# Attention and gated MLP block on one core: chunk ranks, bank-emptying rank, prologue engines and 217 instead of 200 VectorE exponential tiles

## The chip, the cores and the metric

The kernel runs on one core of a Trainium2 chip, in one launch. The metric is the device time of that launch in microseconds (us). A core has a matrix engine (TensorE, PE in the profile), VectorE (DVE), ScalarE (ACT), GpSimd (POOL) and a queue that issues transfers (SyncE, SP). TensorE writes into eight banks of PSUM of 128 x 512 fp32 each, and the other engines empty them.

## The reference

A pre-norm attention block with 32 heads of width 20 over 2048 tokens of width 640, and behind it a gated MLP of width 1728. All inputs are bfloat16.

```python
x = A_x                                   # (1, 2048, 640)
qkv = layernorm(x) @ wqkv                 # 32 heads, Dh = 20
s   = einsum("bhqd,bhkd->bhqk", q, k) * Dh ** -0.5
o   = einsum("bhqk,bhkd->bhqd", softmax(s), v)
h   = x + o.reshape(B, S, D) @ wo
n   = layernorm(h)
out = h + (gelu_tanh(n @ w_gate) * (n @ w_up)) @ w_down
```

## The kernel before

**Scores and exponentials.** The queries are cut into seven chunks of 512, 512, 256, 256, 256, 128 and 128 rows (`CHUNKS`), and the work of a chunk into slots of 64 tiles, 32 slots in all. A tile is 128 keys by 512 columns of scores, one PSUM bank; a group of heads is four heads, whose scores run in four row groups of TensorE. Tiles are put together into units of two or three (`PATS`: a slot marked 2 alternates 3 and 2 banks, a slot marked 3 alternates 3 and 3, and then leaves the background only one bank instead of two). ScalarE takes the exponential of a whole unit in one activation, from 128x1024 or 128x1536, into `pts` or the part of `rege` called `pts2`. `DS` says in hexadecimal how many of a slot's three-tile units give their third tile to VectorE (`d_exp`): one raw step from PSUM per tile, and then seven steps on SBUF for each pair of tiles. The exponentials multiply V on TensorE, accumulated in bank 6, and `epilogue` divides by the sum.

**Behind the attention.** `post` does the rest of a chunk: residual rows of x into `h_sb`, transposed attention output, projection `wo`, LayerNorm (`ln_stats`, `ln_rsqrt`, `ln_apply`), transposes, gates (copied to SBUF, line 1046, then gelu on ScalarE, which needs another activation table than the exponentials), ups (multiplied in line 1058) and downs (added in line 1074, then stored). `h_sb` and the buffer of the gates have room for four tiles of 128 rows: chunks 0 and 1 fill it, chunks 2 and 4 share rows 0 and 1, chunk 3 has rows 2 and 3, chunk 5 row 2 and chunk 6 row 3. The last chunk's `post` is the tail: its gates go from PSUM straight through gelu, line 1032, with ups interleaved in line 1035. The MLP's weights are loaded over the weights of the Q, K and V projections, so after the last of these (`w_readers`).

**What sets the order.** Each operation is recorded with an engine, a planned duration and a rank (line 353 and the other helpers), and `Sched.schedule` then runs a plan: on each engine, among what is ready, the lowest rank first, and within a rank the first recorded. The result is a fixed order for each engine, joined by semaphores. Ranks: scores and their exponentials `P_QK` 0, value products `P_PV` 1, epilogue `P_EPI` 2, background `P_BG` 3, gelu -1, VectorE's seven steps `DPR` 2. All of `post` before the tail has rank 3 (lines 950, 976, 979 and `mms`), so an older chunk's ups and downs, recorded first, go before a younger chunk's projection, LayerNorm and gates. A background operation is put on TensorE only if it ends before a due time, which is when the next unit's scores must start: the later of its banks coming free and ScalarE's coming free less a margin (line 153). Where TensorE would idle for long, the plan puts in a dummy matmul on `gk` (`idle`).

**Prologue.** x comes in four transfers of 512 rows. For each tile of 128 rows LNS says which engine makes the statistics, LNE which one normalizes, LNV which one copies the transposed tile out of PSUM. Group 0's K and Q are then projected (`proj`, ranks G0P, engines G0E for the copy), and V's first half in two banks (`proj_v`).

Of the kernel before, what the change touches and what calls it, by code (L numbers as in the profile page):

```python
# [20 lines left out]
LATE = (0, 1, 2, 3, 4)  # L21
LNS = [{'a': 'act', 'd': 'dve'}[x] for x in 'ddaadddddddaddaa']
LNE = [{'a': 'act', 'd': 'dve'}[x] for x in 'aaaaaaaaddaddddd']
LNV = [{'a': 'act', 'd': 'dve'}[x] for x in 'ddddadaaadaaadad']
SLIP = 0.0
# [25 lines left out]
class Sched:  # L51
# [3 lines left out]
    def __init__(self, nc):  # L55
        self.nc = nc
        self.ops = []
        self.lw = {}
        self.rd = {}

    def op(self, eng, fns, dur, prio, reads=(), writes=(), acq=(), rel=(), after=(), sem=None, lat=None, mode=None, mb=0.0, alt=None):
        o = Op()
        o.i = len(self.ops)
        o.eng, o.dur, o.lat, o.sem = eng, dur, LAT[eng] if lat is None else lat, sem
        o.mode = mode
        o.mb = mb
        o.alt = alt
        o.tag = writes[0] if writes else None
        o.fns = fns if isinstance(fns, list) else [fns]
        o.prio = (prio, o.i)  # L70
        deps = set(after)
        for r in reads:
            if r in self.lw:
                deps.add(self.lw[r])
        for w in writes:
            if w in self.lw:
                deps.add(self.lw[w])
            deps.update(self.rd.get(w, ()))
        for r in reads:
            self.rd.setdefault(r, []).append(o.i)  # L80
        for w in writes:
            self.lw[w] = o.i
            self.rd[w] = []
        deps.discard(o.i)
        o.deps = deps
        o.acq = list(acq)
        o.rel = list(rel)
        o.succ = []
        o.ready = 0.0
        o.start = None  # L90
        o.group = None
        self.ops.append(o)
        return o.i

    def schedule(self):
# [24 lines left out]
        while done < len(ops):  # L120
# [4 lines left out]
            for e in ENGINES:  # L125
# [9 lines left out]
                while ready[e]:  # L135
# [11 lines left out]
                    if got is None:  # L147

                        if p[0] == 0:
                            kept.update(bk.allowed[0] for bk in o.acq)  # L150
                            if e == "pe" and due is None and all(owner[bk.allowed[0]] is None for bk in o.acq):
                                due = max(max(free_at[bk.allowed[0]] for bk in o.acq),
                                          free["act"] - LOOK - o.dur - LAT["pe"])
                        skipped.append((p, i))
                        continue
# [168 lines left out]

P_QK, P_PV, P_EPI, P_BG = 0, 1, 2, 3
TFIRST = 0.0
PRE = 0.0
G0P = (1.5, 2.2, 2.5, 0.5, 2.2)
G0E = [{'a': 'act', 'd': 'dve'}[x] for x in 'aaaad']


def bass_sequential_preLN__mha_block__glu_gated_geglu__prompt_kernel(
# [12 lines left out]
    with ExitStack() as es:  # L345
# [115 lines left out]
        def cst(fn, key, n=128):  # L461
            op(POOL, fn, 0.1 + n * 0.001, P_BG, writes=[key, "pool"])

        cst(I("memset", ident[:], 0.0), "ident")
        cst(I("affine_select", out=ident[:], in_=ident[:], compare_op=ALU.not_equal, fill=1.0,
# [17 lines left out]
        cst(I("memset", e0[:], 0.0), "e0", 1)  # L483
        cst(I("memset", off0[:], 0.0), "off0", 1)
        for j in range(4):
            cst(I("memset", gqh[32 * j:32 * j + 21, 32 * j:32 * j + 1], -0.5), "gqh", 1)
            cst(I("memset", e0[32 * j:32 * j + 1, :], 1.0), "e0", 1)
            cst(I("memset", off0[32 * j:32 * j + 1, :], OFF), "off0", 1)
        pvb0 = Bank(6)
# [4 lines left out]
        def load(dst, src, key, mb, after=(), writes=None):  # L494
            return op("sp", I("dma_start", dst, src), 0.3, P_BG, writes=writes or [key], after=after, sem=key, mb=mb)

        def load_x(i):
            load(x_sb[:, 4 * i:4 * i + 4, :], x_hbm[512 * i:512 * (i + 1), :].rearrange("(t p) d -> p t d", p=128),
                 f"x{i}", 0.65)

# [5 lines left out]

        e_ops = []

        pad_ops = []
# [20 lines left out]
        def ln_stats_act(src, t, rkeys, prio):  # L530
            op("act", I("activation", xn_t[:, t % 2, :], src, ACT.Identity, scale=1.0 / D, accum_out=mv[:, t, 0:1]), 0.65, prio,
               reads=rkeys, writes=[("mv0", t), ("xnj", t % 2)])
            op("act", I("activation", xn_t[:, t % 2, :], src, ACT.Square, bias=mv[:, t, 0:1], scale=-1.0, accum_out=mv[:, t, 1:2]),
               0.65, prio, reads=list(rkeys) + [("mv0", t)], writes=[("mv1", t), ("xnj", t % 2)])

# [40 lines left out]
        def transposes(src, rkeys, dst, wkey, banks, prio, evac, after=(), al=tuple(range(NA)), dma=False, first_=False):  # L576
            if DT and dma:
                aft = tuple(after) + tuple(sc.rd.get(wkey, ()))
                for a in range(NA):
                    op("sp", I("dma_start", dst[:, a, :], src[:, a * 128:(a + 1) * 128], transpose=True), 0.06, prio,  # L580
                       reads=rkeys if len(rkeys) < NG or first_ else rkeys[0:(a * 128 + 127) // 80 + 1], writes=[wkey] if a == NA - 1 else [(wkey, a)], sem=f"t{wkey[1]}", lat=2.6, after=aft)
                return
# [9 lines left out]
            if evac == "act":  # L592
                op("act", lambda eng: eng.activation(dst, v(), ACT.Copy), c_act(128 * len(al)), prio, reads=[key],  # L593
                   writes=[wkey], rel=[bk], after=after)
            else:
                op("dve", lambda eng: eng.tensor_copy(dst, v()), c_dve(128 * len(al)), prio, reads=[key], writes=[wkey],
                   rel=[bk], after=after)
# [10 lines left out]
        for t0 in range(0, NT, 4):  # L608
            sa = [t for t in range(t0, t0 + 4) if LNS[t] == "act"]
            for t in range(t0, t0 + 4):  # L610
                (ln_stats_act if t in sa else ln_stats)(x_sb[:, t, :], t, [f"x{t // 4}"], P_EPI)
            if sa:
                assert sa == list(range(sa[0], sa[-1] + 1))
                op("dve", I("tensor_scalar", mv[:, sa[0]:sa[-1] + 1, 1], mv[:, sa[0]:sa[-1] + 1, 1], 1.0 / D, None, ALU.mult), 0.14,
                   P_QK, reads=[("mv1", t) for t in sa], writes=[("mv", t) for t in sa])
            ln_rsqrt(t0, 4, P_QK, 1)
            for t in range(t0, t0 + 4):
                e_ops.append(ln_apply(LNE[t], x_sb[:, t, :], xn_p[:, t % 4, :], ("xnp", t % 4), t, [f"x{t // 4}"], P_QK))
                transposes(xn_p[:, t % 4, :], [("xnp", t % 4)], xnT[:, :, t * 128:(t + 1) * 128], ("xnT", t),
                           ALLB, P_EPI, LNV[t])  # L620
                e_ops.append(len(sc.ops) - 2)
# [84 lines left out]

        def proj_v(kt, hf, banks, prio, evac="dve"):
            bk = Bank(*banks)
# [9 lines left out]
            else:  # L718
                op("dve", lambda eng: eng.tensor_copy(dst, src()), c_dve(320), prio, reads=[key],  # L719
                   writes=[("v", kt, hf)], rel=[bk])  # L720

# [13 lines left out]

        PATS = '22222222322222232222332222222332'
        DS = '06408846766698a67985888788668802'
        PAT = [((0, 1, 2), (3, 4, 5)) if PATS[i] == '3' else ((0, 1, 2), (3, 4)) for i in range(len(slots))]
# [210 lines left out]
        def post(c, banks, tail):  # L949
            p = P_EPI if tail else P_BG - PRE * (c >= len(CHUNKS) - 2)  # L950
            q0, nq = CHUNKS[c]
# [9 lines left out]
            for tt in range(nt):  # L961
# [7 lines left out]
                else:  # L969
                    transposes(o_nat[:, tt, :], [("on", g) for g in range(NG)], oT[:, :, ht * 128:(ht + 1) * 128],  # L970
                               ("hnT", ht), banks, P_EPI, "dve", after=first, dma=True, first_=c == 0)
                for hf in range(2):
                    bk = Bank(*banks)
                    key = ("bk", sc_id())
                    list(chain(bk, key, 320, [(oT[:, a, ht * 128:(ht + 1) * 128], wo[:, a, hf * 320:(hf + 1) * 320])
                                              for a in range(NA)], [("hnT", ht), "wo"] + [("oTa", ht)] * tail, p))
                    op("dve", lambda eng, bk=bk, ht=ht, hf=hf: eng.tensor_tensor(
# [10 lines left out]
            for tt in range(nt):  # L988
                t = q0 // 128 + tt
                ln_apply("dve", h_sb[:, hb + tt, :], xn_t[:, t % 2, :], ("xn", t % 2), t, [("h", hb + tt, 0), ("h", hb + tt, 1)], p)  # L990
                transposes(xn_t[:, t % 2, :], [("xn", t % 2)], hnT[:, :, (hb + tt) * 128:(hb + tt + 1) * 128], ("hnT", hb + tt),
                           banks, p, "dve", after=first, dma=not tail)
            p, pre = P_BG - TFIRST * tail, p
# [92 lines left out]
        for kt in range(NT):  # L1086
            proj_v(kt, 0, (6, 7), P_BG, "dve")
        ui = 0
        for s_, (c, gs) in enumerate(slots):
            if c == 0:  # L1090
# [5 lines left out]
                if g < 3:  # L1096
                    for kt in range(NT * g // 3, NT * (g + 1) // 3):
                        proj_v(kt, 1, BG0, P_BG)
                if g == 5:
# [60 lines left out]
```

## Time and profile before

| what | value |
|---|---|
| median of 3 runs | 959.46 us (959.09 to 959.96) |
| the profiled execution | 959.65 us |
| its span in the profile | 957.6 us |
| TensorE busy | 888.7 us, 93% |
| ScalarE busy | 910.2 us, 95% |
| VectorE busy | 771.6 us, 81% |
| dummy matmuls on `wo,gk` | 374, 65.7 us |
| ScalarE table loads | 15, 19.2 us |

Times are those of one profiled execution. Records of ScalarE and VectorE overlap their neighbours a little, so the mean length of a record is more than what an instruction adds on a full engine; for that the starts of neighbouring records are compared. In a row of the timeline the columns are start, length, engine, line, operation, output and input, count, and in brackets the idle time before it with what ended it. Where several instructions are merged into one row, the shape shown is that of the first.

### The profile page before, as it was taken

To read this page: it belongs to the slowest core of one execution; us is meant where nothing else is said; L and a number is where in the kernel's file an instruction comes from. 1 tells how busy PE (TensorE), PEld (TensorE's weight loads), DVE (VectorE), ACT (ScalarE), POOL (GpSimd) and SP (SyncE) were. 2 spreads that over 40 slices of the span, in tenths; PEclk is the share of its full clock that TensorE was granted. 3 is DMA by queue.
4 is the path that set the end of the run, shared out by engine and by line. 5 is a ranking of instruction groups with operands and counts; after the bars stand their busy time and mean duration, and the time that the engine had idled before them with its cause. 6 is when DMAs were issued, how large, how long until landed. Compare 5 with 4: busy or idle time off the path is not lost.

```text
span 957.6 us, 33012 instructions
## 1 busy us (share of the span) xinstructions
PE 888.7 (93%) x15035; PEld 391.2 (41%) x15038; DVE 771.6 (81%) x1705; ACT 910.2 (95%) x879; POOL 17.4 (2%) x54
## 2 busy tenths in 40 slices
PE   4999999999999999999999999799999999899998
PEld 2433332232322333233344433334444555655667
DVE  6659758998989998989779989689899978775543
ACT  7799999999999999999999999999999999999931
POOL 4200000000000000000000000000000000000000
PEclk9999999999999999999999999999999999999999
DMA  7000000000000700000001000000110000000000
GB/s 247 2 29 2 2 1 1 2 1 2 1 1 3 262 18 2 1 1 2 9 16 37 2 3 2 1 2 2 30 31 2 3 3 11 24 18 18 4 9 22
DMA packets 11755, 19.88 MB, mean 21 GB/s; under 512 B 544, under 2 KB 9696, under 8 KB 11616
## 3 DMA queue, kind: packets, MB, share of 16 engines
q1 hardware_dynamic: 11616, 17.78, 5.5%
q8 instruction: 118, 1.93, 0.8%
q14 instruction: 21, 0.17, 0.1%
HBM read 15.16 MB, written 2.62 MB: 19 GB/s over the span
## 4 chain that ended last, share of the span: by engine, by line
ACT 90%; PE 7%; DVE 1%; DMA 1%; issue 0%; SPq 0%
ACT pts L353 52%; ACT rege L353 36%; PE ps L632 4%; PE ps L636 1%; ACT L353 1%; PE ps L353 1%; DMA rege<-in_A_x_dram 1%; ACT xn_t L353 0%; DVE rege L353 0%; DVE sq L353 0%; DVE v_all L719 0%; PE ps L586 0%; ACT regw L593 0%; DVE qt_all L667 0%; SPq L353 0%
## 5 line engine op out<-in xcount | busy, mean ns | idle before, releaser
L353 ACT ACTIVATE pts<-ps 128x1024 bf16<-128x1024 f32 (+1 forms) x487 | 555.3, 1357 | 6.5 <-PE ps L353 6.3
L353 ACT ACTIVATE rege<-ps 128x1024 bf16<-128x1024 f32 (+1 forms) x307 | 367.3, 1361 | 2.8 <-PE ps L353 2.8
L353 PE MATMUL ps<-qt_all,kt_all 32*128 32x256 bf16 (+2 forms) x3584 | 310.8, 288 | 36.4 <-ACT pts L353 15.0
L353 PEld LDWEIGHTS ps<-qt_all,kt_all 32*128 32x128 bf16 x3584 | 96.3, 92 | 275.9 <-ACT pts L353 131.5
L636 PE MATMUL ps<-rege,regw 128*32 128x256 bf16 (+2 forms) x2774 | 151.3, 311 | 11.6 <-DVE rege L1058 5.6
L353 PE MATMUL ps<-pts,v_all 128*21 128x256 bf16 (+2 forms) x1984 | 161.9, 291 | 0.0
L353 PE MATMUL ps<-rege,v_all 128*21 128x256 bf16 (+2 forms) x1393 | 125.7, 294 | 0.2 <-ACT rege L353 0.2
L636 PE MATMUL ps<-regw 128*32 128x512 bf16 (+1 forms) x1668 | 119.6, 357 | 0.8 <-DVE qt_all L667 0.4
L353 DVE TENSOR_TENSOR rege<-rege 128x1024 bf16<-128x1024 bf16 (+2 forms) x154 | 101.8, 662 | 1.4
L636 PEld LDWEIGHTS ps<-rege,regw 128*32 128x32 bf16 x2774 | 67.2, 96 | 42.3 <-issue 15.9
L353 DVE TENSOR_SCALAR rege<-rege 128x1024 bf16<-128x1024 int16 (+3 forms) x204 | 81.3, 407 | 1.1
L353 DVE TENSOR_SCALAR qt_all<-ps 128x512 int16<-128x512 f32 x103 | 70.5, 684 | 11.7 <-PE ps L353 10.9
L353 DVE TENSOR_TENSOR qt_all<-qt_all 128x1024 bf16<-128x1024 bf16 (+2 forms) x113 | 76.7, 679 | 0.9
L353 DVE TENSOR_SCALAR rege<-ps 128x512 int16<-128x512 f32 x97 | 66.3, 683 | 11.3 <-PE ps L353 10.7
L353 PEld LDWEIGHTS ps<-pts,v_all 128*21 128x21 bf16 x1984 | 48.5, 90 | 61.3 <-issue 54.0
L636 PE MATMUL ps<-regw,rege 128*32 128x320 bf16 (+1 forms) x1344 | 70.3, 301 | 0.2 <-DVE rege L1058 0.2
L353 DVE TENSOR_SCALAR qt_all<-qt_all 128x1024 bf16<-128x1024 int16 (+2 forms) x166 | 67.6, 413 | 1.1
L353 PE MATMUL ps<-wo,gk 128*21 128x256 bf16 x374 | 65.7, 274 | 0.0
L1058 DVE TENSOR_TENSOR rege<-rege,ps 128x512 bf16<-128x512 bf16 (+2 forms) x53 | 35.9, 678 | 26.6 <-PE ps L636 20.1
L353 PEld LDWEIGHTS ps<-rege,v_all 128*21 128x21 bf16 x1393 | 38.1, 90 | 39.4 <-issue 33.2
L636 PEld LDWEIGHTS ps<-regw 128*32 128x32 bf16 x1668 | 38.4, 95 | 34.8 <-issue 14.8
L1046 DVE CAST rege<-ps 128x512 bf16<-128x512 f32 (+2 forms) x53 | 36.0, 680 | 14.3 <-PE ps L636 14.2
(108 smaller groups left out, 758.9 us busy)
## 6 DMA issues: line engine op xcount, KB each, us to landing
rege<-in_A_x_dram SPq DMA_DIRECT2D x6, 640.0 KB, 5.6
out_dram<-rege SPq DMA_DIRECT2D x16, 160.0 KB, 1.9
regw<-in_B_w_gate_dram SPq DMA_DIRECT2D x1, 2160.0 KB, 9.5
regw<-in_B_w_up_dram SPq DMA_DIRECT2D x1, 2160.0 KB, 14.4
regw<-in_B_w_down_dram SPq DMA_DIRECT2D x1, 2080.0 KB, 19.6
rege<-in_A_wqkv_dram SPq DMA_DIRECT2D x1, 1600.0 KB, 11.5
rege<-in_A_x_dram SPq DMA_DIRECT2D x3, 320.0 KB, 3.3
regw<-in_A_wqkv_dram SPq DMA_DIRECT2D x1, 800.0 KB, 13.1
```

Of the source, the lines that this page charges most:

```text
L353: return lambda eng: getattr(eng, method)(*args, **kwargs)
L632: return [lambda eng: eng.matmul(out()[0:l.shape[-1]], l, r, start=start, stop=stop, skip_group_check=True)]
L636: return [lambda eng, j=j: eng.matmul(out()[j:j + 32], l[:, j:j + 32], r, start=start, stop=stop, tile_position=(0, j), skip_group_check=T ...
L1046: cp.append(op("dve", lambda eng, bg=bg, fv=fv, m=m, w_=w_: eng.tensor_copy(fv, bank(bg, w_)[0:m, :]), c_dve(w_), pre, reads=[kg], writes= ...
L1058: hdone.append(op("dve", lambda eng, bu=bu, fv=fv, m=m, w_=w_: eng.tensor_tensor(fv, fv, bank(bu, w_)[0:m, :], ALU.mult), c_dve(w_), p, re ...
```

## The change

- `PATS` has four slots marked 3 (11, 15, 26, 29) instead of six (8, 15, 20, 21, 29, 30), and `DS` sums to 217 instead of 200. By chunk, the VectorE tiles go from 36, 58, 29, 31, 28, 16, 2 to 42, 57, 29, 34, 27, 16, 12.
- `PRE` is 0.2 and counts for every chunk (`PREC` 0): in `post`, everything up to the gates and their copies has rank 2.8, the ups and downs keep 3.
- After the prologue, VectorE operations that empty a bank and have rank 2 or more get rank 2.5 (`EVP`).
- The due time counts, behind ScalarE's coming free, all exponentials that are ready or known to become so (`HORIZON` 1.0).
- A chunk's output projection waits until its rows of x have come into `h_sb`, before it takes a bank.
- Prologue: x's first 512 rows come in two transfers, `off0` is set first on GpSimd, a square root on it opens ScalarE's work, LNS, LNE, LNV, G0E and G0P are set anew, and V's copies wait for q of group 0, but for the first two tiles. With LNV three instead of eight transposed tiles are copied by ScalarE; LNE keeps nine and LNS five tiles on ScalarE.
- Some planned durations are corrected. The paths with `dma` stay unused, as `DT` is 0.

```diff
-LNS = [{'a': 'act', 'd': 'dve'}[x] for x in 'ddaadddddddaddaa']
-LNE = [{'a': 'act', 'd': 'dve'}[x] for x in 'aaaaaaaaddaddddd']
-LNV = [{'a': 'act', 'd': 'dve'}[x] for x in 'ddddadaaadaaadad']
+LNS = [{'a': 'act', 'd': 'dve'}[x] for x in 'dddadddadddaddaa']
+LNE = [{'a': 'act', 'd': 'dve'}[x] for x in 'adaadaaaadadaddd']
+LNV = [{'a': 'act', 'd': 'dve'}[x] for x in 'ddddaddddddaddad']
...
+        if self.evp is not None and eng == "dve" and rel and prio >= P_EPI:
+            prio = self.evp
...
                                 due = max(max(free_at[bk.allowed[0]] for bk in o.acq),
-                                          free["act"] - LOOK - o.dur - LAT["pe"])
+                                          free["act"] + HORIZON * sum(ops[x[-1]].dur for x in ready["act"] + future["act"]
+                                                                      if ops[x[-1]].prio[0] == P_QK) - LOOK - o.dur - LAT["pe"])
...
+HORIZON = 1.0
+EVP = 2.5
+PREC = 0
+VH = 2
-PRE = 0.0
-G0P = (1.5, 2.2, 2.5, 0.5, 2.2)
-G0E = [{'a': 'act', 'd': 'dve'}[x] for x in 'aaaad']
+PRE = 0.2
+G0P = (2.5, 2.5, 2.5, 2.2, 2.2)
+G0E = [{'a': 'act', 'd': 'dve'}[x] for x in 'aadaa']
...
+        cst(I("memset", off0[:], 0.0), "off0", 1)
+        for j in range(4):
+            cst(I("memset", off0[32 * j:32 * j + 1, :], OFF), "off0", 1)
...
         def load_x(i):
-            load(x_sb[:, 4 * i:4 * i + 4, :], x_hbm[512 * i:512 * (i + 1), :].rearrange("(t p) d -> p t d", p=128),
-                 f"x{i}", 0.65)
+            for t0, n in ((0, 2), (2, 2)) if i == 0 else ((4 * i, 4),):
+                load(x_sb[:, t0:t0 + n, :], x_hbm[128 * t0:128 * (t0 + n), :].rearrange("(t p) d -> p t d", p=128),
+                     xkey(t0), 0.16 * n)
...
+        op("act", I("activation", nm[:, 0:1], off0[:], ACT.Sqrt), 0.06, -1, mode="sqrt", reads=["off0"], writes=["pre", ("nm", 0)])
...
-        PATS = '22222222322222232222332222222332'
-        DS = '06408846766698a67985888788668802'
+        PATS = '22222222222322232222222222322322'
+        DS = '06518868658678897868898988658866'
...
-            p = P_EPI if tail else P_BG - PRE * (c >= len(CHUNKS) - 2)
+            p = P_EPI if tail else P_BG - PRE * (c >= PREC)
...
-                                              for a in range(NA)], [("hnT", ht), "wo"] + [("oTa", ht)] * tail, p))
+                                              for a in range(NA)], [("hnT", ht), "wo"] + [("oTa", ht)] * tail, p, after=(sc.lw["h", ht, hf],)))
...
-            proj_v(kt, 0, (6, 7), P_BG, "dve")
+            proj_v(kt, 0, (6, 7), P_BG, "dve", after=(sc.lw["q", 0, 0],) if kt >= VH else ())
+        sc.evp = EVP if EVP >= 0 else None
...
-                        proj_v(kt, 1, BG0, P_BG)
+                        proj_v(kt, 1, BG0, P_BG, after=(sc.lw["q", 0, 0],))
```

More of the change, by code (lines that the diff above doesn't have):

```diff
@@ L59, in __init__ @@
         self.rd = {}
+        self.evp = None
     def op(self, eng, fns, dur, prio, reads=(), writes=(), acq=(), rel=(), after=(), sem=None, lat=None, mode=None, mb=0.0, alt=None):
+        if self.evp is not None and eng == "dve" and rel and prio >= P_EPI:
+            prio = self.evp
         o = Op()
@@ L325 @@
 P_QK, P_PV, P_EPI, P_BG = 0, 1, 2, 3
+DTO = ''
+DTH = ''
+HORIZON = 1.0
+EVP = 2.5
+PREC = 0
+VH = 2
 TFIRST = 0.0
-PRE = 0.0
-G0P = (1.5, 2.2, 2.5, 0.5, 2.2)
-G0E = [{'a': 'act', 'd': 'dve'}[x] for x in 'aaaad']
+PRE = 0.2
+G0P = (2.5, 2.5, 2.5, 2.2, 2.2)
+G0E = [{'a': 'act', 'd': 'dve'}[x] for x in 'aadaa']
 def bass_sequential_preLN__mha_block__glu_gated_geglu__prompt_kernel(
@@ L483, in bass_sequential_preLN__mha_block__glu_gated_geglu__prompt_kernel @@
         cst(I("memset", e0[:], 0.0), "e0", 1)
-        cst(I("memset", off0[:], 0.0), "off0", 1)
         for j in range(4):
@@ L487, in bass_sequential_preLN__mha_block__glu_gated_geglu__prompt_kernel @@
             cst(I("memset", e0[32 * j:32 * j + 1, :], 1.0), "e0", 1)
-            cst(I("memset", off0[32 * j:32 * j + 1, :], OFF), "off0", 1)
         pvb0 = Bank(6)
@@ L495, in load, with xkey @@
             return op("sp", I("dma_start", dst, src), 0.3, P_BG, writes=writes or [key], after=after, sem=key, mb=mb)
+        def xkey(t):
+            return f"x{t // 4}" if t >= 2 else "x00"
         def load_x(i):
-            load(x_sb[:, 4 * i:4 * i + 4, :], x_hbm[512 * i:512 * (i + 1), :].rearrange("(t p) d -> p t d", p=128),
-                 f"x{i}", 0.65)
+            for t0, n in ((0, 2), (2, 2)) if i == 0 else ((4 * i, 4),):
+                load(x_sb[:, t0:t0 + n, :], x_hbm[128 * t0:128 * (t0 + n), :].rearrange("(t p) d -> p t d", p=128),
+                     xkey(t0), 0.16 * n)
         for i in range(4):
@@ L530, in ln_stats_act @@
         def ln_stats_act(src, t, rkeys, prio):
-            op("act", I("activation", xn_t[:, t % 2, :], src, ACT.Identity, scale=1.0 / D, accum_out=mv[:, t, 0:1]), 0.65, prio,
+            op("act", I("activation", xn_t[:, t % 2, :], src, ACT.Identity, scale=1.0 / D, accum_out=mv[:, t, 0:1]), 0.73, prio,
                reads=rkeys, writes=[("mv0", t), ("xnj", t % 2)])
             op("act", I("activation", xn_t[:, t % 2, :], src, ACT.Square, bias=mv[:, t, 0:1], scale=-1.0, accum_out=mv[:, t, 1:2]),
-               0.65, prio, reads=list(rkeys) + [("mv0", t)], writes=[("mv1", t), ("xnj", t % 2)])
+               0.82, prio, reads=list(rkeys) + [("mv0", t)], writes=[("mv1", t), ("xnj", t % 2)])
         def ln_rsqrt(t0, n, prio, need_nm=False):
@@ L579, in transposes @@
                 for a in range(NA):
-                    op("sp", I("dma_start", dst[:, a, :], src[:, a * 128:(a + 1) * 128], transpose=True), 0.06, prio,
-                       reads=rkeys if len(rkeys) < NG or first_ else rkeys[0:(a * 128 + 127) // 80 + 1], writes=[wkey] if a == NA - 1 else [(wkey, a)], sem=f"t{wkey[1]}", lat=2.6, after=aft)
+                    op("sp", I("dma_start", dst[:, a, :], src[:, a * 128:(a + 1) * 128], transpose=True), 1.27, prio,
+                       reads=rkeys if len(rkeys) < NG or first_ else rkeys[0:(a * 128 + 127) // 80 + 1], writes=[wkey] if a == NA - 1 else [(wkey, a)], sem=f"t{wkey[1]}", lat=1.3, after=aft)
                 return
@@ L595, in transposes @@
             else:
-                op("dve", lambda eng: eng.tensor_copy(dst, v()), c_dve(128 * len(al)), prio, reads=[key], writes=[wkey],
+                op("dve", lambda eng: eng.tensor_copy(dst, v()), c_dve(128 * len(al), 0.52), prio, reads=[key], writes=[wkey],
                    rel=[bk], after=after)
@@ L610, in bass_sequential_preLN__mha_block__glu_gated_geglu__prompt_kernel @@
             for t in range(t0, t0 + 4):
-                (ln_stats_act if t in sa else ln_stats)(x_sb[:, t, :], t, [f"x{t // 4}"], P_EPI)
+                (ln_stats_act if t in sa else ln_stats)(x_sb[:, t, :], t, [xkey(t)], P_EPI)
             if sa:
@@ L617, in bass_sequential_preLN__mha_block__glu_gated_geglu__prompt_kernel @@
             for t in range(t0, t0 + 4):
-                e_ops.append(ln_apply(LNE[t], x_sb[:, t, :], xn_p[:, t % 4, :], ("xnp", t % 4), t, [f"x{t // 4}"], P_QK))
+                e_ops.append(ln_apply(LNE[t], x_sb[:, t, :], xn_p[:, t % 4, :], ("xnp", t % 4), t, [xkey(t)], P_QK))
                 transposes(xn_p[:, t % 4, :], [("xnp", t % 4)], xnT[:, :, t * 128:(t + 1) * 128], ("xnT", t),
@@ L705, in proj, with proj_v @@
                reads=[key2, ("kh", g), (nm, g, c)], writes=[(nm, g, c)], rel=[b2])
-        def proj_v(kt, hf, banks, prio, evac="dve"):
+        def proj_v(kt, hf, banks, prio, evac="dve", after=()):
             bk = Bank(*banks)
@@ L719, in proj_v @@
                 op("dve", lambda eng: eng.tensor_copy(dst, src()), c_dve(320), prio, reads=[key],
-                   writes=[("v", kt, hf)], rel=[bk])
+                   writes=[("v", kt, hf)], rel=[bk], after=after)
         slots = []
@@ L970, in post @@
                     transposes(o_nat[:, tt, :], [("on", g) for g in range(NG)], oT[:, :, ht * 128:(ht + 1) * 128],
-                               ("hnT", ht), banks, P_EPI, "dve", after=first, dma=True, first_=c == 0)
+                               ("hnT", ht), banks, P_EPI, "dve", after=first, dma=str(c) in DTO, first_=c == 0)
                 for hf in range(2):
@@ L991, in post @@
                 transposes(xn_t[:, t % 2, :], [("xn", t % 2)], hnT[:, :, (hb + tt) * 128:(hb + tt + 1) * 128], ("hnT", hb + tt),
-                           banks, p, "dve", after=first, dma=not tail)
+                           banks, p, "dve", after=first, dma=str(c) in DTH)
             p, pre = P_BG - TFIRST * tail, p
```

## The prediction

> **What bounds the kernel now.** I read the page first (busy times, chain), then ScalarE's instructions by form, then stages, then the end and the beginning instruction by instruction.
>
> ```profile
> PE 888.7 (93%) x15035; PEld 391.2 (41%) x15038; DVE 771.6 (81%) x1705; ACT 910.2 (95%) x879; POOL 17.4 (2%) x54
> ...
> ACT 90%; PE 7%; DVE 1%; DMA 1%; issue 0%; SPq 0%
> ```
>
> Nine tenths of the chain is ScalarE. The stages, with the columns stage, length and busy time of PE, PEld, DVE, ACT, POOL, show that TensorE is hardly freer:
>
> ```profile
> 60.00:330.00 270.00, 256.52 (x3190) 82.46 (x3187) 231.99 (x495) 269.28 (x256) 0.00 (x0) 1.00 0.06 20
> 330.00:660.00 330.00, 306.44 (x4487) 117.17 (x4483) 286.77 (x609) 329.76 (x313) 0.00 (x0) 1.00 0.04 13
> 660.00:913.00 253.00, 239.64 (x6249) 137.72 (x6247) 195.31 (x449) 252.54 (x232) 0.00 (x0) 1.00 0.05 14
> 913.00:957.60 44.60, 41.25 (x534) 31.54 (x534) 18.96 (x39) 9.79 (x13) 0.00 (x0) 1.00 0.05 16
> ```
>
> From 60 to 913 us ScalarE never rests. After 913 it is idle and TensorE is full: it works off what it could not place between the scores. So there are two bounds in a row. The end, first ScalarE, then TensorE:
>
> ```profile
> 904.46 1.28 ACT L353 ACT_TABLE_LOAD   x1
> 905.76 3.29 ACT L353 ACTIVATE rege<-rege 128x2048 bf16<-128x2048 bf16 x2
> 909.06 1.28 ACT L353 ACT_TABLE_LOAD   x1
> ...
> 915.54 1.45 ACT L353 ACTIVATE rege<-ps 128x1536 bf16<-128x1536 f32 x1 [2.82 <-PE ps L353]
> 916.89 1.02 ACT L353 ACTIVATE pts<-ps 128x1024 bf16<-128x1024 f32 x1
> ...
> 934.46 1.70 ACT L353 ACTIVATE rege<-rege 128x1792 bf16<-128x1792 bf16 x1 [5.67 <-DVE rege L1046]
> ```
>
> ```profile
> 928.66 0.44 PE L586 MATMUL ps<-ident,xn_t 128*128 128x128 bf16 x5
> ...
> 933.50 8.11 PE L632 MATMUL ps<-rege,regw 128*64 128x128 bf16 x136
> 941.45 4.28 PE L632 MATMUL ps<-regw,rege 128*128 128x320 bf16 x28
> 945.66 4.92 PE L632 MATMUL ps<-rege,regw 128*128 128x128 bf16 x79
> 950.52 4.29 PE L632 MATMUL ps<-regw,rege 128*128 128x320 bf16 x28
> ...
> 954.85 0.49 DVE L1074 TENSOR_TENSOR rege<-ps,rege 128x320 bf16<-128x320 f32 x1 [1.20 <-PE ps L632]
> ```
>
> The last exponential ends at 916.89 + 1.02 = 917.9. The 1792-wide gelu at 934.46 is chunk 5's (14 blocks of 128 columns), so even chunk 5 is unfinished, and its work stands among chunk 6's. What must follow the last exponential is only chunk 6: its normalized rows are transposed by 929.1, I allow 0.5 for the copy, half of the 8.11 for its gates (4.1; the other half is chunk 5's), 4.9 for its ups, 4.3 for its downs, and 957.6 - 954.85 = 2.75 for the last addition and store. That is 945.65, **27.7 us behind the last exponential**. The 12.0 us above it are older work.
>
> **The model of the end.** While older work is left, a shorter ScalarE phase merely moves it behind the last exponential: scores and value products still take their full TensorE time. Therefore end = 957.6 - prologue gain - R, where R is TensorE time that is now idle or spent on dummy matmuls and gets used for real work. It can't be earlier than the new last exponential + 27.7.
>
> **The change, part by part.** 217 instead of 200 tiles on VectorE, 4 instead of 6 slots with 3+3 units. Counting PATS and DS through the unit loop gives 794 units before, 803 after: 226 activations of 1536 (260 before), 576 of 1024 (534), one of 512. The trace has the same 260 (156 + 104) and 534 (331 + 203):
>
> ```profile
> L353 ACT ACTIVATE pts<-ps 128x1024 bf16<-128x1024 f32 x331 | 355.0, 1216 | 0.7 <-PE ps L353 0.7
> L353 ACT ACTIVATE pts<-ps 128x1536 bf16<-128x1536 f32 x156 | 251.0, 1658 | 5.8 <-PE ps L353 5.6
> L353 ACT ACTIVATE rege<-ps 128x1024 bf16<-128x1024 f32 x203 | 223.4, 1209 | 0.0
> L353 ACT ACTIVATE rege<-ps 128x1536 bf16<-128x1536 f32 x104 | 168.5, 1659 | 2.8 <-PE ps L353 2.8
> ```
>
> Those means overlap their neighbours. The price on a full engine is from start to start:
>
> ```profile
> 409.09 1.33 ACT L353 ACTIVATE pts<-ps 128x1024 bf16<-128x1024 f32 x1
> 409.99 2.68 ACT L353 ACTIVATE rege<-ps 128x1536 bf16<-128x1536 f32 x2
> ...
> 854.53 3.07 ACT L353 ACTIVATE rege<-ps 128x1536 bf16<-128x1536 f32 x2
> 857.19 1.75 ACT L353 ACTIVATE pts<-ps 128x1536 bf16<-128x1536 f32 x1
> ```
>
> 0.90 for 1024, 2.66 / 2 = 1.33 for 1536, so 0.47 for 512. ScalarE saves 34 x 1.33 - 42 x 0.90 - 0.47 = **7.0 us**. VectorE pays per tile one raw step and per pair three products and four scalar steps:
>
> ```profile
> L353 DVE TENSOR_SCALAR rege<-ps 128x512 int16<-128x512 f32 x97 | 66.3, 683 | 11.3 <-PE ps L353 10.7
> L353 DVE TENSOR_TENSOR rege<-rege 128x1024 bf16<-128x1024 bf16 x110 | 75.2, 684 | 1.1
> L353 DVE TENSOR_SCALAR rege<-rege 128x1024 bf16<-128x1024 int16 x110 | 45.8, 417 | 0.6
> ```
>
> 17 x 0.683 + 10 pairs x (3 x 0.684 + 4 x 0.417) = 49 us at most (three of the pairs are halves). Ten of the tiles go to chunk 6, six to chunk 0, three to chunk 3, and others lose two. VectorE is at 195.3 of 253 us in the last stage, at 232 of 270 in the first, so this is covered; uncovered it is the third rival.
>
> Ranks. A chunk's output projection, LayerNorm and gates (PRE 0.2, PREC 0: rank 2.8) now go ahead of older ups and downs (rank 3). Chunk 0 is the clearest case. The down weights are ordered only after the last projection, and chunk 0's LayerNorm runs after that too, with TensorE on dummies. First the DMA and the first gate matmuls; then stage, length and busy time, in the first row of gk's matmuls alone, in the others of all of TensorE:
>
> ```profile
> 317.22 0.37 SPq L353 DMA_DIRECT2D regw<-in_B_w_gate_dram  x1
> ...
> 350.67 1.05 PE L636 MATMUL ps<-rege,regw 128*32 128x512 bf16 x16
> ```
>
> ```profile
> 320.00:350.00 30.00, 5.94 (x33) 1.00 0.57 212
> ...
> 320.00:350.00 30.00, 27.58 (x314) 1.00 0.57 212
> 900.00:920.00 20.00, 16.23 (x586) 1.00 0.02 4
> ```
>
> 5.94 + 2.42 = 8.4 us of that window are lost; with LayerNorm done before the weights land I take 6 back. In the last hole (3.8 us of 900 to 920, where ScalarE also waits 2.82 us for scores) I take 3. Chunk 4's front beside chunk 3's back, a second background bank in two more slots, rank 2.5 for bank-emptying VectorE work and the later due time (HORIZON) together: 3 us of the remaining idle time (13.4 us in 660 to 913). **R = 12**; bounds 0 and the floor below. What speaks for the lower end: chunk 1 needs all four rows of h_sb and can't start before chunk 0 is finished, and chunk 5 shares its row with chunk 3. If chunk 5's gelu now falls among the exponentials, it costs ScalarE two loads and itself, 1.29 + 1.70 + 1.29 and 0.3 to empty the pipe: 4.6 us. By the rows a load is followed by the next activation in 0.02 us (904.46 + 1.28 to 905.76). The Trainium skill (ScalarE: Activation LUTs, What ACT_TABLE_LOAD costs) puts a drain of 1.38 us beside each load, 2.66 us a switch; no row here shows it, and by it this gelu would cost 2.8 us more.
>
> Prologue:
>
> ```profile
> 0.75 2.91 SPq L353 DMA_DIRECT2D rege<-in_A_x_dram  x4
> ...
> 10.13 1.28 ACT L353 ACT_TABLE_LOAD   x1
> ...
> 25.32 2.45 ACT L593 ACTIVATE regw<-ps 128x640 bf16<-128x640 bf16 x4
> ...
> 36.66 2.37 ACT L353 ACTIVATE pts<-ps 128x1536 bf16<-128x1536 f32 x2 [4.39 <-PE ps L353]
> ```
>
> ```profile
> 29.70 0.48 DVE L719 CAST v_all<-ps 128x320 bf16<-128x320 f32 x1
> 30.10 0.58 DVE L353 TENSOR_TENSOR sq<-kt_all 128x512 bf16<-128x512 bf16 x1
> ```
>
> Off ScalarE go five transposed tiles (8 to 3; 2.45 / 4 = 0.61 each, 3.1) and the table load at 10.13, which now happens while x is under way (1.28). V's copies beyond the first two wait until q is ready: of the six that stand on VectorE between 29.7 and 35.5, four leave, 0.40 each, 1.6. Behind those copies wait only V's two banks and, later, the value products. Against it: five copies more on VectorE (2.0) and a fifth x DMA on SP ahead of the weights (2.91 / 4 = 0.7). Bounds 0 (VectorE takes the place) and 3.1 + 1.28 + 1.6 = 6.0; the first two tiles landing earlier is left as reserve. I take **3.0**.
>
> **The sum.** 957.6 - 3.0 - 12 = 942.6. The floor: last exponential at 917.9 - 3.0 - 7.0 - 2.8 + 4.6 = 909.7, plus 27.7 = 937.4, so it doesn't bind. The profiled execution took 959.65, 2.05 more than its span, and the median is 0.19 lower: 942.6 + 2.05 - 0.2 = **944.5 us**.
>
> **Rivals.** (1) TensorE's holes stay, because rows of h_sb, not ranks, set the order, and VectorE's extra 49 us keep the banks full: R between 0 and 3. End 957.6 - 3.0 - 1.5 = 953.1, 955.0 us; at R = 0 and a prologue gain under 2 it is no change. For it: rows shared by chunks. Against it: the window from 320 to 350. (2) The ranks do more than I took: the floor, 937.4 + 1.9 = 939.3. It lies in my range. (3) Slower: the due time is set by all exponentials in hand, so a background matmul may run until ScalarE is nearly dry; where the chip is behind the plan, scores come late. Once this costs 0.03 us at each of 803 units, it is 24 us: last exponential at 909.7 + 24 = 933.7, plus 27.7 and 1.9: 963.3. It decides from about 0.028 a unit, 22 us. For it: the 2.82 us wait at 915.54 is one such. Against it: ScalarE's 0.7 and 0.0 us of idle time before the 534 short exponentials show no such wait in 870 us now, and more TensorE work gets in meanwhile. (4) Each table switch also drains: 4.6 becomes 7.4, and the last exponential is 2.8 later, floor 942.1 after adding 1.9; it would bind only if R were over 14. The Trainium skill's page named above says so; the rows don't.
>
> **How the numbers follow.** Forecast with (2): 0.66. (1): 0.18, of which 0.04 is no change. (3): 0.09. (4): 0.01. What I didn't think of: 0.06, half faster, a third the same. A measurement of this kernel tells 0.2% from no change, 1.9 us. Faster 0.66 + 0.14 + 0.01 + 0.03 = 0.84; same 0.06; slower 0.10. The range 936 to 957 leaves out (3), the no-change part of (1) and a few per cent below.
>
> **What would show it.** Right: 217 raw steps on VectorE; 226 and 576 long and short exponentials; the first exponential near 33.7; few gk matmuls between 320 and 350; the last exponential near 910; less than 10 us of chunk 4's and 5's work behind it. Wrong: ScalarE idle in many small pieces between 60 and 900 (3); as much older work as before at the end (1); a first exponential still at 36 (VectorE bounds the prologue).

## The result and the profile after

| | before | changed |
|---|---|---|
| median, same chip | 959.51 us (959.09 to 959.96, 4 runs) | 944.51 us (943.99 to 945.13, 4 runs) |
| span of the profiled execution | 957.6 us | 941.8 us |
| last exponential ends | 917.9 us | 914.5 us |
| from there to the end (tail) | 39.7 us | 27.3 us |
| TensorE idle + dummies, 60 us to last exponential | 51.0 + 65.7 = 116.7 us | 41.9 + 52.7 = 94.6 us |

The ratio is 0.9844, 95% interval 0.9827 to 0.9861, so the changed kernel is 1.6% faster. The page of the changed kernel, busy times, chain and dummies:

```profile
PE 882.1 (94%) x15332; PEld 387.8 (41%) x15334; DVE 806.4 (86%) x1798; ACT 902.9 (96%) x885; POOL 18.0 (2%) x54
...
ACT 75%; PE 14%; DVE 10%; DMA 1%; issue 0%; SPq 0%
...
L363 PE MATMUL ps<-wo,gk 128*21 128x256 bf16 x297 | 52.7, 274 | 0.0
```

VectorE works 34.8 us more (771.6 before; the prediction allowed 49 at most for the tiles) and ScalarE 7.3 us less. The chain is no longer ScalarE's alone: a quarter of it is work of TensorE and VectorE. ScalarE's exponentials by form, in the changed kernel:

```profile
L363 ACT ACTIVATE pts<-ps 128x1024 bf16<-128x1024 f32 x349 | 371.1, 1210 | 3.4 <-PE ps L363 3.2
L363 ACT ACTIVATE rege<-ps 128x1024 bf16<-128x1024 f32 x227 | 246.0, 1210 | 0.4 <-PE ps L363 0.3
L363 ACT ACTIVATE pts<-ps 128x1536 bf16<-128x1536 f32 x141 | 228.2, 1634 | 5.7 <-PE ps L363 5.7
L363 ACT ACTIVATE rege<-ps 128x1536 bf16<-128x1536 f32 x85 | 137.0, 1633 | 0.0
...
L363 ACT ACTIVATE pts<-ps 128x512 bf16<-128x512 f32 x1 | 0.6, 597 | 0.0
```

349 + 227 = 576 short ones, 141 + 85 = 226 long ones and one of 512, as counted. VectorE's raw steps are 217, also as counted. The end, ScalarE's timeline of the changed kernel (start, length):

```profile
885.14 1.97 ACT L363 ACTIVATE rege<-ps 128x1024 bf16<-128x1024 f32 x2 [0.28 <-PE ps L363]
...
896.32 1.94 ACT L363 ACTIVATE pts<-ps 128x1024 bf16<-128x1024 f32 x2 [0.87 <-PE ps L363]
898.27 1.28 ACT L363 ACT_TABLE_LOAD   x1
899.57 1.70 ACT L363 ACTIVATE rege<-rege 128x1792 bf16<-128x1792 bf16 x1
901.28 1.28 ACT L363 ACT_TABLE_LOAD   x1
902.57 1.94 ACT L363 ACTIVATE rege<-ps 128x1024 bf16<-128x1024 f32 x2
904.89 4.46 ACT L363 ACTIVATE pts<-ps 128x1536 bf16<-128x1536 f32 x4 [0.38 <-PE ps L363]
...
911.53 2.94 ACT L363 ACTIVATE pts<-ps 128x1536 bf16<-128x1536 f32 x3
914.49 1.28 ACT L363 ACT_TABLE_LOAD   x1
```

Chunk 5's gelu (1792 wide) now falls among the exponentials and costs 902.57 - 898.27 = 4.30 us there. The wait of 2.82 us has gone, but three small ones have come, 0.28 + 0.87 + 0.38 = 1.53 us together. The tail, TensorE's timeline of the changed kernel:

```profile
921.52 4.04 PE L648 MATMUL ps<-regw,rege 128*128 128x320 bf16 x27
...
926.42 8.33 PE L648 MATMUL ps<-rege,regw 128*128 128x128 bf16 x140 [0.35 <-DVE rege L612]
934.69 4.29 PE L648 MATMUL ps<-regw,rege 128*128 128x320 bf16 x28
```

From 926.4 on only chunk 6's gates, ups and downs run. Chunk 5's downs (921.52) fill the time of chunk 6's LayerNorm. Behind the last exponential TensorE still does 51 matmuls of ups and 38 of downs of chunks 4 and 5, at about 0.06 and 0.15 us some 9 us, under the 10 that the prediction named. None of them stands among chunk 6's gates, ups and downs.

**Where TensorE got its time.** Stage, length and busy time, first of gk's matmuls, then of all of TensorE, in the kernel before:

```profile
350.00:470.00 120.00, 12.65 (x73) 1.00 0.01 3
...
570.00:660.00 90.00, 6.30 (x44) 1.00 0.01 2
...
350.00:470.00 120.00, 112.50 (x1324) 1.00 0.01 3
...
570.00:660.00 90.00, 80.48 (x1335) 1.00 0.01 2
```

and in the changed one, all of TensorE first, then gk's:

```profile
320.00:350.00 30.00, 25.74 (x289) 1.00 0.62 223
350.00:470.00 120.00, 114.82 (x1546) 1.00 0.02 6
570.00:660.00 90.00, 86.42 (x1577) 1.00 0.04 11
...
320.00:350.00 30.00, 3.88 (x18) 1.00 0.62 223
350.00:470.00 120.00, 4.50 (x28) 1.00 0.02 6
570.00:660.00 90.00, 5.44 (x30) 1.00 0.04 11
```

In 350 to 470 us, 7.5 + 12.65 = 20.2 us were lost and are now 5.2 + 4.5 = 9.7; in 570 to 660 us, 9.5 + 6.3 = 15.8 are now 3.6 + 5.4 = 9.0. Those two make 17.3 of the 22.1 us. The stages are fixed times, so the work in them is not the same in both kernels. In 320 to 350 us, where the prediction looked for half of it, 4.26 + 3.88 = 8.1 us are lost, as 8.4 before.

**The link between the chunks.** Chunk 1's rows of x can be loaded only when chunk 0's downs have left `h_sb`. SP's queue, before:

```profile
509.51 0.39 SPq L353 DMA_DIRECT2D rege<-in_A_x_dram  x1
```

and in the changed kernel, with the first of the MLP's weights:

```profile
327.42 0.37 SPq L363 DMA_DIRECT2D regw<-in_B_w_gate_dram  x1
...
469.09 0.39 SPq L363 DMA_DIRECT2D rege<-in_A_x_dram  x1
```

Chunk 0 is finished 40 us earlier, though its weights are ordered 10 us later (317.22 before). Chunk 1's background starts where chunk 0's ends. In the changed kernel the lead is kept: the five later loads of rows of x, for chunks 2 to 6, are issued 28 to 53 us earlier than before (chunk 4's at 778.7 instead of 814.8).

### The profile page after: what moved, and what is told of

It reads as the page before. It is cut to its first block, busy times and chain, and to the rows that moved or that the text cites. A ratio compares the mean times of both kernels' runs of the same rounds, so it can differ in the third digit from the quotient of the medians.

```text
span 941.8 us, 33723 instructions
## 1 busy us (share of the span) xinstructions
PE 882.1 (94%) x15332; PEld 387.8 (41%) x15334; DVE 806.4 (86%) x1798; ACT 902.9 (96%) x885; POOL 18.0 (2%) x54
## 4 chain that ended last, share of the span: by engine, by line
ACT 75%; PE 14%; DVE 10%; DMA 1%; issue 0%; SPq 0%
ACT pts L363 44%; ACT rege L363 30%; PE ps L652 5%; PE ps L363 5%; DVE rege L363 3%; PE ps L648 3%; DVE qt_all L363 2%; DVE rege L1062 1%; DMA rege<-in_A_x_dram 1%; DVE rege L1074 1%; PE ps L602 1%; DVE stats L363 1%; ACT L363 1%; DVE rege L612 0%; DVE sq L363 0%
## 5 line engine op out<-in xcount | busy, mean ns | idle before, releaser
L652 PE MATMUL ps<-rege,regw 128*32 128x256 bf16 (+2 forms) x3046 | 161.1, 306 | 6.0 <-ACT rege L363 3.0
L363 DVE TENSOR_TENSOR rege<-rege 128x1024 bf16<-128x1024 bf16 (+2 forms) x173 | 113.6, 660 | 0.9
L363 DVE TENSOR_SCALAR rege<-rege 128x1024 bf16<-128x1024 int16 (+3 forms) x229 | 91.3, 408 | 1.6
L652 PEld LDWEIGHTS ps<-rege,regw 128*32 128x32 bf16 x3046 | 74.0, 96 | 39.4 <-issue 15.1
L363 DVE TENSOR_SCALAR qt_all<-ps 128x512 int16<-128x512 f32 x110 | 75.4, 686 | 10.8 <-PE ps L363 10.4
L363 DVE TENSOR_TENSOR qt_all<-qt_all 128x1024 bf16<-128x1024 bf16 (+3 forms) x121 | 80.8, 668 | 1.0
L363 DVE TENSOR_SCALAR rege<-ps 128x512 int16<-128x512 f32 x107 | 73.3, 685 | 9.6 <-PE ps L363 9.1
L652 PE MATMUL ps<-regw,rege 128*32 128x320 bf16 x1524 | 77.1, 301 | 0.7 <-DVE rege L1074 0.5
L363 DVE TENSOR_SCALAR qt_all<-qt_all 128x1024 int16<-128x1024 int16 (+3 forms) x178 | 71.7, 411 | 1.2
L363 PE MATMUL ps<-wo,gk 128*21 128x256 bf16 x297 | 52.7, 274 | 0.0
L652 PEld LDWEIGHTS ps<-regw,rege 128*32 128x32 bf16 x1524 | 36.5, 95 | 23.8 <-issue 12.5
## 6 DMA issues: line engine op xcount, KB each, us to landing
regw<-in_B_w_up_dram SPq DMA_DIRECT2D x1, 2160.0 KB, 13.3
rege<-in_A_wqkv_dram SPq DMA_DIRECT2D x1, 1600.0 KB, 12.7
```

The costliest lines, as they stand in the source:

```text
L363: return lambda eng: getattr(eng, method)(*args, **kwargs)
L652: return [lambda eng, j=j: eng.matmul(out()[j:j + 32], l[:, j:j + 32], r, start=start, stop=stop, tile_position=(0, j), skip_group_check=T ...
```

## The experiments

Every kernel was timed beside the kernel before. The columns after the ratio are from its profiled execution: end of the last exponential, tail, TensorE idle + dummies from 60 us to the last exponential, the issue of the gate weights, the issue of chunk 1's rows of x (SP's rows as above), and the first and last copy of chunk 0's 14 gates on VectorE (line 1046 before).

| kernel | time us | ratio, 95% interval | last exp. | tail | lost | weights | chunk 1's x | chunk 0's gates |
|---|---|---|---|---|---|---|---|---|
| before | 959.1 to 959.5 | | 917.9 | 39.7 | 116.7 | 317 | 509.5 | 354 to 412 |
| changed | 944.51 | 0.9844 (0.9827 to 0.9861) | 914.5 | 27.3 | 94.6 | 327 | 469.1 | 342 to 384 |
| before + tiles | 961.74 | 1.0026 (1.0017 to 1.0036) | 906.5 | 53.3 | 117.2 | 323 | 522.5 | 381 to 427 |
| before + ranks | 962.03 | 1.0026 (1.0016 to 1.0036) | 917.5 | 42.4 | 123.0 | 345 | 521.6 | 357 to 421 |
| before + ranks + tiles | 958.88 | 0.9995 (0.9986 to 1.0004) | 911.5 | 45.2 | 113.7 | 359 | 509.5 | 373 to 419 |
| before + due time | 958.96 | 0.9995 (0.9986 to 1.0005) | 917.3 | 39.6 | 116.4 | 317 | 508.8 | 355 to 421 |
| before + bank rank | 962.51 | 1.0032 (1.0021 to 1.0044) | 913.7 | 47.0 | 122.3 | 317 | 540.3 | 357 to 436 |
| before + three | 959.11 | 0.9999 (0.9989 to 1.0008) | 913.8 | 43.0 | 112.9 | 347 | 509.7 | 360 to 410 |
| changed - bank rank | 960.13 | 1.0012 (0.9997 to 1.0027) | 911.6 | 44.2 | 114.1 | 358 | 508.3 | 371 to 417 |
| changed - ranks | 962.10 | 1.0030 (1.0017 to 1.0043) | 903.7 | 56.3 | 115.5 | 316 | 506.9 | 359 to 407 |
| changed - tiles | 957.19 | 0.9983 (0.9973 to 0.9993) | 925.2 | 29.7 | 115.0 | 325 | 494.6 | 340 to 394 |
| changed - due time | 951.43 | 0.9915 (0.9901 to 0.9930) | 909.3 | 39.6 | 102.3 | 331 | 491.0 | 345 to 389 |
| changed, digits swapped | 944.05 | 0.9839 (0.9824 to 0.9853) | 914.2 | 27.3 | 95.1 | 327 | 469.1 | 342 to 389 |
| changed, late gelu | 945.09 | 0.9842 (0.9826 to 0.9859) | 910.6 | 31.9 | 95.1 | 327 | 469.1 | 342 to 384 |

The end of the last exponential can be compared between two runs only where the same gelus stand ahead of it. Chunk 4's costs ScalarE 5.9 us there with its two loads (904.46 to 910.34 before), chunk 5's 4.3. The changed kernel, the one with two digits swapped and the one with the old tiles have both ahead of it. "Before + tiles", "before + bank rank" and "changed - ranks" have neither. All others have chunk 4's alone.

**The new tiles alone** (in the kernel before).

```diff
-        PATS = '22222222322222232222332222222332'
-        DS = '06408846766698a67985888788668802'
+        PATS = '22222222222322232222222222322322'
+        DS = '06518868658678897868898988658866'
```

> The kernel before with only the new PATS and DS (217 VectorE tiles). Theory A (two bounds in a row: while TensorE has older work left behind the last exponential, a shorter ScalarE phase only moves that work): the last exponential ends up to 7 us earlier, the older work behind it grows by about as much, time 957 to 960 us. Rival B (ScalarE alone sets the time): 7.0 us less, 952.5 us. Rival C (VectorE too full): over 961 us.

ScalarE's timeline of that run:

```profile
903.45 3.00 ACT L353 ACTIVATE pts<-ps 128x1536 bf16<-128x1536 f32 x3
906.47 1.28 ACT L353 ACT_TABLE_LOAD   x1
...
912.70 3.28 ACT L353 ACTIVATE rege<-rege 128x2048 bf16<-128x2048 bf16 x2
```

The last exponential ends 11.4 us earlier, and the time is 2.5 us longer; the tail grows from 39.7 to 53.3 us. Of the 11.4 us, 5.9 are chunk 4's gelu, which now stands behind it (912.70), so 5.5 are left for the tiles. The stage table of the same run, to the end:

```profile
906.00:959.70 53.70, 49.15 (x557) 38.29 (x554) 26.28 (x64) 13.73 (x16) 0.00 (x0) 1.00 0.04 14
```

TensorE is busy for 49 of these 53.7 us. A shorter ScalarE phase only moved work behind it: theory A's mechanism, and against B. By its number, 961.7 us, the run lies above A's 960 and within C's bound. C's mechanism is not seen, as the exponentials were not held up; why the time is longer instead of the same stays open.

**The ranks alone.**

```diff
-            p = P_EPI if tail else P_BG - PRE * (c >= len(CHUNKS) - 2)
+            p = P_EPI if tail else P_BG - 0.2
...
-                                              for a in range(NA)], [("hnT", ht), "wo"] + [("oTa", ht)] * tail, p))
+                                              for a in range(NA)], [("hnT", ht), "wo"] + [("oTa", ht)] * tail, p, after=(sc.lw["h", ht, hf],)))
```

> The kernel before with only the new ranks (2.8 for projection, LayerNorm and gates of every chunk before the tail) and the output projection's wait for its rows of x. Theory A: TensorE gets 6 to 12 us more real work done before the last exponential, no older work but what fills chunk 6's LayerNorm is left, and the time falls to last exponential + 27.7 us: 947 us if chunk 5's gelu stays behind the last exponential, 952 us if it falls among the exponentials (4.6 us more on ScalarE). Rival B: no gain, 959.5 us or up to 4.6 us more.

962.0 us, against theory A, and by the number within rival B's bounds (959.5 and up to 4.6 more). But B's reason for more is not what happened: chunk 5's gelu stays behind the last exponential, which ends at 917.5 as before, and it is the tail that grows. Chunk 0's projection begins at 268 instead of 308 us (the first addition of line 977), but the last Q projections give way to it, so that the last of their matmuls starts at 344.5 instead of 316.4 us, and the weights, which wait for them, are ordered at 345 instead of 317 us. So what was won ahead of the weights seems to have been lost in waiting for them.

**Ranks and tiles together** (both edits above).

> The kernel before with the new ranks and the new PATS and DS together. Theory A: with the older work gone, ScalarE's 7.0 us count in full: 7 us below the run with ranks alone, 940 to 946 us. Rival B: 7 us below before, 952.5 us, whatever the ranks.

Both numbers fail: no gain over the kernel before, 3.2 us below the run with ranks alone, and the weights are ordered at 359 us.

**The later due time alone.**

```diff
-                                          free["act"] - LOOK - o.dur - LAT["pe"])
+                                          free["act"] + HORIZON * sum(ops[x[-1]].dur for x in ready["act"] + future["act"]
+                                                                      if ops[x[-1]].prio[0] == P_QK) - LOOK - o.dur - LAT["pe"])
```

> The kernel before with only the later due time (HORIZON 1.0). Theory A: some dummy matmuls are replaced by real work, 3 us or less are won, 956 to 960 us. Rival D (scores come late wherever the chip is behind the plan): ScalarE waits in many small pieces between 60 and 900 us, time above 961 us.

No change that can be measured, within A's bounds. ScalarE doesn't get late: its last exponential ends at 917.3 against 917.9. D is out here.

**The bank-emptying rank alone.**

```diff
+        if self.evp is not None and eng == "dve" and rel and prio >= P_EPI:
+            prio = self.evp
...
+        sc.evp = 2.5
```

> The kernel before with only the rank 2.5 for bank-emptying VectorE operations. Theory E (the bank-emptying rank is what gives TensorE its time back, above all in 330 to 660 us, where the changed kernel has 7 us less idle time and 13 us fewer dummies): the older work behind the last exponential falls by up to 12 us, time 947 to 955 us, dummies well below 65 us. Rival F (it needs the ranks of the chunks beside it): 957 to 960 us.

Worse than both expectations: 962.5 us, with 122 us lost on TensorE and the latest chunk 1 of all runs.

**The changed kernel without that rank** (`EVP = -1`).

> The changed kernel without the rank 2.5 for bank-emptying VectorE operations. Theory E: older work stands behind the last exponential again, tail well over 27 us, dummies back over 60 us, time 950 to 958 us. Rival G (what gives it is the prologue's or the tiles' share): 944 to 947 us.

The tail is 44.2 us and the dummies are at 65.0 us, as theory E said, with 960.1 us a little above its bounds. The last Q projection's matmuls start at 356.9 instead of 327.0 us, and the weights are ordered at 358 us, 30 us later than with it. So in the whole kernel this rank keeps the ranks from putting off the Q projections; alone it gains nothing.

**The changed kernel without the ranks** (`PRE = 0.0`).

> The changed kernel with PRE 0, so projection, LayerNorm and gates have rank 3 again. Theory E with the ranks as a small share (as the run with ranks alone showed no gain): 944 to 949 us. Theory A (the ranks are needed): 951 us or more, with a tail of over 32 us.

962.1 us: the ranks are needed, theory A's branch. The timeline of ScalarE in this run:

```profile
900.65 3.04 ACT L363 ACTIVATE pts<-ps 128x1536 bf16<-128x1536 f32 x3
903.70 1.28 ACT L363 ACT_TABLE_LOAD   x1
...
916.37 3.28 ACT L363 ACTIVATE rege<-rege 128x2048 bf16<-128x2048 bf16 x2 [1.88 <-DVE rege L1062]
```

It has the earliest last exponential of all runs, 10.8 us ahead of the changed kernel, and one of the latest ends, 56.3 us behind it. Of the 10.8 us, 5.9 + 4.3 = 10.2 are the two gelus that the changed kernel has ahead of it: ScalarE is not really faster here, it only has its gelus still to do.

**The changed kernel with the old tiles** (`PATS` and `DS` of before).

> The changed kernel with the old PATS and DS (200 tiles). If the changed kernel's end is set by its last exponential + 27.3 us, ScalarE's 7.0 us count in full: 951.5 us, with the tail still 27 to 28 us. If TensorE's older work sets it, the exponentials don't count: 944 to 946 us.

957.2 us, 12.7 more instead of 7.0. The tail is short (29.7), so the end follows the last exponential, but that one is 10.7 us later: besides the tiles' 7.0 us ScalarE waits 13.3 instead of 9.2 us for scores. Chunk 0's gates take 54 instead of 42 us. They do so in each pair of runs that differ by the tiles: 58 and 46 before, 64 and 46 with the ranks.

**Three parts together** (ranks, bank rank and tiles in the kernel before).

> The kernel before with three parts: ranks 2.8, bank-emptying rank 2.5 and the new PATS and DS; prologue, due time and planned durations as before. Theory H (a serial chain: the ranks bring chunk 0's projection and LayerNorm ahead of the weights, the bank-emptying rank keeps the last Q projections, and so the weights, from being put off, the new tiles shorten chunk 0's gates; each is lost without the others): chunk 0's gates start near 342 us, its downs end near 470, the tail is 27 to 30 us, time 945 to 949 us. Rival K (PATS, DS and the prologue's choices fit the one complete plan, and any other plan falls back): 954 to 962 us.

959.1 us: theory H falls, and the number is rival K's. Chunk 0's projection and LayerNorm are early, its gates take 50 us, and yet the weights are ordered at 347 us. SP's queue of this run:

```profile
347.35 0.37 SPq L356 DMA_DIRECT2D regw<-in_B_w_gate_dram  x1
...
509.67 0.39 SPq L356 DMA_DIRECT2D rege<-in_A_x_dram  x1
```

What the three lack against the changed kernel is the due time, the prologue's choices, the waits of V's copies and the corrected planned durations.

**Two digits of DS swapped** in the changed kernel.

```diff
-        DS = '06518868658678897868898988658866'
+        DS = '06518868658687897868898988658866'
```

> The changed kernel with two neighbouring digits of DS swapped (slots 12 and 13, 7 and 8 tiles become 8 and 7), all sums the same. Theory H: 943 to 947 us. Rival K (the plan is brittle, and a part's removal costs 13 to 18 us because the plan becomes another one): 950 us or more.

944.05 us. The plan is not brittle in this direction, against rival K. Chunk 0's gates, which run beside slot 12, end 5 us later with the one tile more there, and chunk 1's x is still issued at 469.1, so chunk 0's ups and downs make up for it.

**The changed kernel without the due time** (`HORIZON = 0.0`).

> The changed kernel with the due time of before (HORIZON 0). Theory H: 944 to 948 us, since the later due time alone won nothing. Rival D (the later due time makes scores late): less ScalarE waiting and under 943 us. Rival K: 950 us or more.

951.4 us, 6.9 more: over H's 948 and within rival K's bound of 950 or more, though K's reason, a brittle plan, was not seen in the swap. Rival D is out: the time is longer, not shorter. The last exponential ends 5.2 us earlier, but 4.3 of these are chunk 5's gelu, which now stands behind it. Chunk 1's x comes at 491 us, and the tail is 39.6 us. What gains nothing in the kernel before is worth 7 us here.

**Chunk 5's gelu behind the last exponential.**

```diff
+                if c == len(CHUNKS) - 2:
+                    late_gelu.extend(gl)
...
+                if tail:
+                    for i_ in late_gelu:
+                        sc.ops[i_].deps.add(last_exp[0])
```

> The changed kernel with chunk 5's gelu put behind the last exponential, so that ScalarE's two table loads and the gelu (1.28 + 1.70 + 1.28 us at 898 to 902.6) leave the exponentials. If the end is the last exponential + 27.3 us and the tail has TensorE room for chunk 5's ups and downs: last exponential near 910, time 940 to 942 us. If chunk 5's ups and downs then push chunk 6 back: 944 to 949 us.

ScalarE's timeline of this run:

```profile
907.67 2.92 ACT L363 ACTIVATE pts<-ps 128x1536 bf16<-128x1536 f32 x3
910.61 1.28 ACT L363 ACT_TABLE_LOAD   x1
911.90 1.70 ACT L363 ACTIVATE rege<-rege 128x1792 bf16<-128x1792 bf16 x1
```

The last exponential ends 3.9 us earlier, and the time is the same (945.1 us), the second of the two expectations. From 910.0 us to the end at 942.5 TensorE is busy for 29.2 of 32.5 us, so it has no room for more of chunk 5's work. So in the changed kernel too, this shorter ScalarE phase gains nothing by itself.

## Why the number was right, and which steps were not

The time came out at the forecast 944.5 us, but not by the sum as written; two of its steps were off, in opposite directions.

- **Two bounds in a row.** Right, and shown: in the run with tiles alone ScalarE's exponentials end earlier (5.5 us by the tiles themselves) and the time does not fall. Moving chunk 5's gelu shows the same in the changed kernel.
- **ScalarE's 7.0 us.** The counts came out. As a gain they exist only where no older work is left, as the model said; in the kernel before they were worth nothing (tiles alone: 2.5 us slower).
- **Prologue, 3.0 us.** Measured 36.66 - 34.52 = 2.14, and then it was given back. ScalarE and VectorE in the changed kernel:

```profile
34.52 2.37 ACT L363 ACTIVATE pts<-ps 128x1536 bf16<-128x1536 f32 x2 [3.86 <-PE ps L363]
...
66.80 4.20 ACT L363 ACTIVATE pts<-ps 128x1024 bf16<-128x1024 f32 x4 [2.14 <-PE ps L363]
```

```profile
65.44 0.74 DVE L719 SCALAR_TENSOR_TENSOR qt_all<-ps,khalf,qt_all 128x512 bf16<-128x512 f32 x1
```

  The wait at 66.80 stands where the next slot begins and needs group 1's q, which VectorE finishes at 66.2. The kernel before has no such wait there:

```profile
66.16 4.49 ACT L353 ACTIVATE pts<-ps 128x1024 bf16<-128x1024 f32 x4
```

  In the kernel before, the same step of VectorE ends at 63.8 us. So the exponentials start 2.1 us earlier, and the next group's q comes 2.4 us later. V's copies that now wait behind group 0's q are a likely cause, as VectorE does three of them between 62 and 65.5 us; no run tested it. An earlier start must be followed to the next thing that the engine needs; this step wasn't in the prediction.
- **The last exponential at 909.7.** Measured 914.5. Of the 4.8 us, the first exponential explains 0.9, the wait at 66.80 another 2.1, and the small waits at the end 1.5. Chunk 5's gelu was 4.3 instead of 4.6. Some 0.6 us are left open.
- **R = 12 us, so that the floor doesn't bind.** This is the step that failed, in its size and its place. TensorE loses 22 us less. Of the 6 us that I took from 320 to 350 us nothing came. I held the shared rows of `h_sb` against the change; the runs speak for the opposite, that chunk 0's earlier end moves chunk 1 and what follows. Runs with an earlier issue of chunk 1's x are faster: 469.1 us goes with 944 to 945, 491.0 with 951.4, 494.6 with 957.2, and 507 to 540 with 959 to 962.5. That this is the cause is argued, not shown. No run moved this event alone, within the last group it does not order the times (506.9 us goes with 962.1), and in the kernel without the due time the lead is gone by chunk 4's rows (817.7 against 814.8 before) and yet it is 8 us faster than before.
- **The floor itself.** Right: 27.7 us were worked out, 27.3 measured. So the end is rival (2)'s mechanism, with a last exponential 4.8 us later than worked out. That the two errors, a later last exponential and a floor that binds, sum to the forecast is chance.
- **What each part brings.** Wrong: I gave shares of R to single parts. None of the four parts that were run alone gains (tiles, ranks, bank rank: 2.5 to 3.5 us slower; due time: no change), three together gain nothing, and taking one out of the whole costs 6.9 to 17.6 us. By the table, the tiles go with shorter gates of chunk 0, the ranks with an early projection, and the bank rank, in the whole kernel, with weights that aren't put off.
- **Rival (1)** is what all the partial kernels do but the one without the due time: 113 to 123 us lost, 957 to 962.5 us, where it said 955. **Rival (3)** did not happen: ScalarE waits 9.2 us for scores in the changed kernel and 8.8 without the later due time, nothing like 24. **Rival (4)** is not seen: 1.30 + 1.71 + 1.29 us from the first load to the next exponential leave no place for a drain of 1.38 us beside each load.

Open is how the last 14.6 us between the three parts together and the changed kernel divide. The due time has 6.9 of them when it is left out of the whole. If that is its share, the other 7.7 lie among the prologue's engines and ranks, the waits of V's copies and the corrected durations; these were not run one by one. Why the three parts together still order the weights 20 us late is open with it. That fewer VectorE tiles beside chunk 0's gates are what shortens them is argued from the pairs of runs and the swap, not shown by itself. The prologue's changes were never run alone.

## What to carry to other kernels

Before an engine that is always busy is relieved, look at what stands behind its last instruction: if another engine works on there, the saving is only moved. In a kernel whose order comes from a planner, parts can't be priced one at a time; run each alone and each left out, and watch one early event that the rest seems to hang on (here the load of chunk 1's rows). When two runs are compared by the end of one engine's phase, the same work must stand ahead of it in both. Follow an earlier start to the next operand the engine needs.

## What the hardware showed

Pulling older work out of the tail isn't free on TensorE. Forms of TensorE's matmuls in the kernel before, the downs between the scores and in the tail:

```profile
L636 PE MATMUL ps<-regw,rege 128*32 128x320 bf16 x1248 | 64.4, 301 | 0.2 <-DVE rege L1058 0.2
...
L632 PE MATMUL ps<-regw,rege 128*128 128x320 bf16 x104 | 15.5, 300 | 0.0
```

Between the scores a step is four matmuls on column quarters, 4 x 64.4 / 1248 = 0.206 us; in the tail it is one on the whole array, 15.5 / 104 = 0.149 us, 28% less. In the changed kernel the first form has 1416 matmuls and the second 62, so 42 steps of downs went from the one way to the other. TensorE's whole span can be added up: work, dummies and idle time are 823.0 + 65.7 + 68.9 = 957.6 us before and 829.4 + 52.7 + 59.7 = 941.8 us in the changed kernel. It loses 22.2 us less over the whole span and works 6.4 us more, and the difference is the 15.8 us by which the span fell. By the two rows above, the 42 steps account for some 42 x (0.206 - 0.149) = 2.4 of the 6.4 us, an estimate; gates and ups moved in the same way, but were not priced.
